# Six tiles of a chunked linear-attention stage in 64x64 matmul tiles, with their loads split by even and odd heads and the decay tables on GpSimd

## The chip, the cores and the metric

The kernel runs on one core of one Trainium2 chip. The time is the device time of one execution in microseconds (us). The engines are named as in the profile: PE is TensorE (matmuls), PEld its loading of weights, DVE is VectorE, ACT is ScalarE, POOL is GpSimd, and SP is SyncE, which only issues DMAs. L316 is line 316 of the kernel before; a line of the changed kernel is named as such.

## The reference

Two stages follow each other. The first is a linear attention with decay over 768 tokens, for 4 batches and 8 heads of 64 dimensions; the second is a feed-forward layer with a sine inside, on all 3072 tokens:

```python
gamma = 1.0 - 2.0 ** (-5.0 - np.arange(H))          # one decay per head
for t in range(S):
    state = gamma * state + outer(k[t], v[t])        # (64 x 64) per batch and head
    y[t] = scale * q[t] @ state
...
x = y as (3072 tokens, 512)                          # heads side by side
h = x @ w_in                                         # 512 -> 2048
g = h + sin(alpha * h) ** 2 / alpha
out = g @ w_out                                      # 2048 -> 512
```

Inputs and output are float32; the matmuls work on bf16.

## The kernel before

**Tiles.** The attention is computed in chunks of 128 tokens: 6 per batch, 24 tiles in all. Inside a chunk the decay is brought into tables, so that three kinds of matmul remain: *scores* (keys times queries, masked to the causal half), *values* (masked scores times values, plus queries times the state that the earlier chunks left), and the *state* (keys times values, added to the running sum). The order of the 24 tiles is written out: first the four first chunks of the four batches (tiles 1 to 4), then batch by batch the other five chunks. So tiles 5 to 9 are chunks two to six of batch 0, tile 10 is the second chunk of batch 1, and the 14 tiles from 11 on are all later ones. They go to the second stage in eleven groups: the first four tiles together, then two at a time.

**Two ways to compute a tile.** Tiles 11 to 24 are *wide*: their queries, keys and values lie with 64 tokens on each half of the partitions, four heads on each half, and all their matmuls are 64x64 (64 rows of contraction, 64 output rows), four of which fit into the PE array. `burst` (L391) issues them: `inter` (queries times state, L344), `scores` of the next tile (L355, L359), `sums` (the state, L374) and `mix` (values, L387). `mix` adds into the same PSUM as `inter` from other array rows, so an empty PE instruction in front of it waits for the last product of `inter`. DVE then masks the next tile's scores (L364), takes the outputs out with the decay table (`leave`, L414) and adds the state to its float sum (`keep`, L421); ACT, or POOL in batch 3, copies that sum to bf16 for the next tile (`hand`, L427).

Tiles 5 to 10 are not wide: all 128 tokens lie on the partitions. `stage_A` (L267) gives scores in 8 matmuls of 64 rows by 128 output rows (L273), and one DVE operation masks them (L277). `stage_M` (L305) multiplies queries with a block-diagonal copy of the state (`s_bd`, 128 rows by 64, L316), adds the values (L320) and, in `stage_S` (L280), adds the state into one PSUM bank that keeps it from tile to tile (L287). DVE takes the output out (L327, one operation of 128x512), and ACT copies the state's two diagonal blocks to `s_bd` (L303). When the first wide tile follows, `turned` (L291) changes the places of the heads in the state.

**Loads.** Every chunk load is issued by POOL (L84: 128 tokens x 8 heads x 64, cast to bf16 on the way), each of q, k and v by itself, and so are the weights (`w_in` in four pieces, L119; `w_out` in four, L122) and the wide tiles' loads, one per head (L109). The order in which POOL issues them is written out in the program. Queries and keys are turned by PE for the first tiles and for tiles 5, 6 and 8 (`stage_T`, L254; copied out by ACT or DVE), for the other tiles by a DMA transposition that SP issues (`turn`, L264). The values are scaled with their decay by `scale_v` (L143), on DVE for tiles 5 and 6 and on POOL for the others.

**Decay tables.** `qg` has a table of 128x512 floats for each chunk number; ACT makes the first, and `decay_table` (L220) multiplies it into the other five on DVE: three at 14.9 us, one each in slots 0 and 4 of phase 1.

**Second stage and order.** A `Slot` (L442) is a group of first-layer products: for a group of two tiles 8 products of 256 columns (L456), ACT's two sines (L459), a square on ACT (L464) or DVE (L466), and DVE's two additions into `gT` (L471). The products with `w_out` (L481, *output products*) follow one group later. `phase(g)` runs the eight slots of group g; in each slot it issues the slot's products, then what the dictionary `atts` has put there for attention tiles, then some output products of the group before, then the additions. Each engine takes its own instructions in that order. In PSUM, the slots and the output products share four banks (tag "mm"), and the attention's outputs have the banks "ps" and "ty".

Group 0 is written out by hand with tiles 4, 5 and 6 in it. There `fill(n)` issues n output products, 32 of which remain for the tiles 3 and 4: 16 are placed before phase 1 and 16 in it. Before phase 1 stand the scores of tiles 5 and 6, the first state (`SK(e0)`), and `stage_M` of both. In phase 1, slot 0 has tile 8's transposition, slot 1 tile 7's scores, slot 3 tile 7's `stage_M` and tile 8's scores, slot 6 tile 8's and tile 9's. Phase 2 has tile 9 in slot 1, with the scores of tile 10 and the first state of batch 1, and tile 10 in slot 5 with the first wide scores.

Of the kernel before, what the change touches and what calls it, by code (L numbers as in the profile page):

```python
# [8 lines left out]
F32 = mybir.dt.float32  # L9
# [7 lines left out]
def kernel(  # L17
# [15 lines left out]
    nc = tc.nc  # L33
# [35 lines left out]

    def chunk_of(t, j):  # L70
        b, c = divmod(j, NCH)
        return t[b, :, c * C:(c + 1) * C, :].rearrange("h s d -> s h d")

    def load_chunk(j, names="qkv"):
        for name, src in (("q", q), ("k", k), ("v", v)):
# [8 lines left out]
            nc.gpsimd.dma_start(out=t, in_=chunk_of(src, j))  # L84
# [4 lines left out]

    def spot(h):  # L90

        return h // NP, (h % NP) ^ (h // NP)

    def load_seq(bt, names="qkv"):
# [7 lines left out]
        for name, src in (("q", q), ("k", k), ("v", v)):  # L102
            if name not in names:
                continue
            for h in range(H):
                b, at = spot(h)
                r = slice(64 * b, 64 * b + 64)
                o = tv[r, :, at, :] if name == "v" else tqk[r, :, "qk".index(name), at, :]
                nc.gpsimd.dma_start(out=o, in_=src[bt, h, cs[0] * C:, :].rearrange("(f i) d -> i f d", i=64))  # L109
# [44 lines left out]
    load_w_in(3)  # L154
    load_w_out(2)
    load_w_out(3)
    for j in order[4:7]:
        load_chunk(j)
# [36 lines left out]
    def later_tables():  # L195
        for b in range(2):
# [3 lines left out]
            for e in range(2):  # L200
                nc.vector.tensor_copy(lgq[r, e::2], lg[r, NP * b + (e ^ b):NP * b + NP:2])
# [17 lines left out]
    def decay_table(c):  # L219
        nc.vector.tensor_mul(qg[:, c], qg[:, 0], step[:, c, :, None].to_broadcast([128, NP, C]))  # L220
# [5 lines left out]
    s_bd = [big.tile([128, NP, 128], BF16, name=f"s_bd{i}") for i in range(2)]  # L226
# [53 lines left out]
    def stage_S(j):  # L280
        c = j % NCH
        if c == 0:
            st["ps"] = psum.tile([128, NP, D], F32, name="ps", tag="ps")
        ps = st["ps"]
        for p in range(NP):
            for e in range(2):
                nc.tensor.matmul(ps[64 * e:64 * e + 64, p, :], raw["k", j][:, 2 * p + e, :], raw["v", j][:, 2 * p + e, :],  # L287
                                 start=(c == 0 and p == 0), stop=True, skip_group_check=True)
        return ps

    def turned(to, ps, copy):  # L291

        copy(to[:, 0:2], ps[:, 0:2])
        for e in range(2):
            copy(to[64 * e:64 * e + 64, 2:4], ps[64 - 64 * e:128 - 64 * e, 2:4])

    def keep_S(j, ps):
        if wide(j + 1):
            turned(s_q[(j % NCH + 1) % 2], ps, nc.scalar.copy)
            return  # L300
        for e in range(2):
            r = slice(64 * e, 64 * e + 64)
            nc.scalar.copy(s_bd[(j % NCH + 1) % 2][r, :, r], ps[r, :, :])  # L303

    def stage_M(j):  # L305
        c = j % NCH
# [3 lines left out]
        qkT, aT, vs = st["qkT", j], st["aT", j], raw["v", j]  # L310
        py = psum.tile([128, NP, 128], F32, name="py", tag="ty")
        if c > 0:
            for p in range(NP):
                for e in range(2):
                    r = slice(64 * e, 64 * e + 64)
                    nc.tensor.matmul(py[r, p, :], s_bd[c % 2][:, p, r], qkT[:, p, :],  # L316
                                     start=(p == 0), stop=True, skip_group_check=True)
        for p in range(NP):
            for e in range(2):
                nc.tensor.matmul(py[64 * e:64 * e + 64, p, :], vs[:, 2 * p + e, :], aT[:, e, p, :],  # L320
                                 start=(c == 0 and p == 0), stop=True, skip_group_check=True)
        x = xT[g][:, :, i * C:(i + 1) * C]
        if c == 0:
            nc.scalar.copy(x, py)
            return
        ps = stage_S(j) if c < NCH - 1 else None
        nc.vector.tensor_mul(x, py, qg[:, c])  # L327
        if ps is not None:
            keep_S(j, ps)

    def half(x):
        return slice(64 * x, 64 * x + 64)
# [3 lines left out]
    def inter(j):  # L338
# [3 lines left out]
        for m in range(2):  # L342
            for b, e in tiles4:
                last = nc.tensor.matmul(st["py", j][b][half(e ^ b), m * 128:(m + 1) * 128].rearrange("p (f i) -> p f i", f=2),  # L344
                                        s[half(e), 2 * b + m, :], qkT[half(e), m:m + 5:4, half(b)],
                                        start=(m == 0), stop=True, skip_group_check=True)
        return last

    def scores(j):

        qkT = st["qkT", j]
        pa = st["pa", j] = psum.tile([128, 2, 512], F32, name="pa", tag="pa")
        for m in range(2):
# [8 lines left out]
        aT = work.tile([128, 2, 2, 192], BF16, name="aTw", tag="aT", bufs=2)  # L362
        st["aT", j] = aT
# [3 lines left out]
    def sums(now, to, lo):  # L367

        ks, vs = raw["k", now], raw["v", now]
        for f in range(2 if wide(now) else 1):  # L370
            for m in range(2):
                for b, e in tiles4:
                    h = 4 * b + 2 * m + (e ^ b)
                    nc.tensor.matmul(to[b][half(e), lo + 64 * m:lo + 64 + 64 * m],  # L374
                                     ks[half(b), f, 2 * m + e, :] if wide(now) else ks[:, h, :],
                                     vs[half(b), f, 2 * m + e, :] if wide(now) else vs[:, h, :],
# [435 lines left out]
```

## Time and profile before

| | us |
|---|---|
| median of 3 runs | 213.54 (213.53 to 214.42) |
| profiled execution, of which | 213.53 |
| its span | 211.7 |
| phase 1 with the first slot of phase 2 | 48.10 to 63.97 |
| the next eight slots | 63.97 to 79.34 |
| the eight after them | 79.34 to 95.04 |

A line of the timeline has a start in us from the span's start, the busy time, the engine, the line of the kernel, the operation, output <- inputs, partitions x elements with their types, and the number of instructions that were merged; in brackets stands how long the engine was idle ahead of it and what it waited for. For PE, a name such as 64\*128 is rows by columns of the array that a matmul takes. A busy time of several merged matmuls runs to the end of the last one, while the next may start behind the last one's start. In a row of busy time by stage stand the stretch, its length, and the busy times of PE, PEld, DVE, ACT and POOL with their instruction counts, then the granted clock of PE, the DMA share and GB/s. The granted clock is 1.00 all through.

### The profile page before, as it was taken

What the parts mean: (1) busy time and instruction counts of PE and PEld (TensorE: products, weight loads), DVE (VectorE), ACT (ScalarE), POOL (GpSimd) and SP (SyncE); (2) the same over time, 40 slices, a digit from 0 to 9 for tenths busy, and PEclk for the clock granted to TensorE, in tenths of its full rate; (3) what the DMA queues carried; (4) which work ended last, traced back from release to release, by engine and by line L of the source; (5) the groups of instructions that cost most, each with busy time, mean ns of one, the idle gap of its engine ahead of it and who ended that gap; (6) DMA issues with size and microseconds to landing.
All of it is one profiled execution on the core that took longest, in us unless ns stands there. A gap on an engine that the chain in (4) does not pass through costs nothing.

```text
span 211.7 us, 5581 instructions
## 1 busy us (share of the span) xinstructions
PE 199.4 (94%) x2227; PEld 131.0 (62%) x2253; DVE 155.7 (74%) x353; ACT 157.7 (74%) x339; POOL 105.2 (50%) x140
## 2 busy tenths in 40 slices
PE   7798899899989999999999999999999999999994
PEld 3345454457766766766666667666666666666653
DVE  5877849966997688687777787777777878666550
ACT  7588696858887887877867877876876786788821
POOL 8975434977989649699799951001021020000000
PEclk9999999999999999999999999999999999999999
DMA  8999999999997989999999994403513110110112
GB/s 124 154 198 186 206 207 173 154 148 240 142 152 71 166 129 159 113 133 140 140 182 167 193 127 104 99 24 79 88 38 81 54 48 5 50 50 3 50 50 99
DMA packets 101337, 25.00 MB, mean 118 GB/s; under 512 B 93872, under 2 KB 98368, under 8 KB 101312
## 3 DMA queue, kind: packets, MB, share of 16 engines
q0 software_dynamic: 77504, 13.38, 86.7%
q1 hardware_dynamic: 23664, 11.22, 26.3%
q8 instruction: 17, 0.28, 0.6%
q14 instruction: 8, 0.07, 0.1%
q10 hardware_dynamic: 144, 0.07, 0.1%
HBM read 27.27 MB, written 6.29 MB: 159 GB/s over the span
## 4 chain that ended last, share of the span: by engine, by line
PE 78%; DVE 14%; ACT 4%; issue 3%; ACTq 0%
PE po L481 33%; PE ph L456 31%; DVE gT L471 5%; DVE aT L277 4%; PE spare L525 3%; ACT s L459 2%; ACT s L464 2%; PE poh L506 2%; PE py L344 2%; PE py L387 1%; DVE s L466 1%; PE pa L273 1%; PE pa L355 1%; PE py L320 1%; PE pa L374 1%
## 5 line engine op out<-in xcount | busy, mean ns | idle before, releaser
L471 DVE SCALAR_TENSOR_TENSOR gT<-s,rec_alpha,ph 128x256 bf16<-128x256 f32 (+3 forms) x184 | 82.4, 489 | 36.0 <-ACT s L464 35.8
L459 ACT ACTIVATE s<-ph,alpha_sb 128x256 f32<-128x256 f32 (+3 forms) x184 | 79.3, 480 | 35.2 <-PE ph L456 34.5
L456 PE MATMUL ph<-xT,w_in 128*128 128x256 bf16 (+3 forms) x735 | 98.6, 277 | 0.3 <-DVE gT L471 0.2
L481 PE MATMUL po<-w_out,gT 128*128 128x512 bf16 x344 | 90.4, 379 | 4.8 <-issue 3.3
L456 PEld LDWEIGHTS <-w_in 128*128 128x128 bf16 x736 | 70.6, 98 | 30.6 <-issue 1.0
L464 ACT ACTIVATE s<-s 128x512 f32<-128x512 f32 (+1 forms) x92 | 57.1, 621 | 2.5
L481 PEld LDWEIGHTS <-gT 128*128 128x128 bf16 x368 | 33.8, 98 | 27.7 <-issue 1.2
L427 POOL CAST s_q<-s_f 128x256 bf16<-128x256 f32 x5 | 2.0, 397 | 43.3 <-DVE s_f L421 25.7
L143 POOL TENSOR_TENSOR v_seq<-v_seq,kgq 128x512 bf16<-128x512 bf16 x14 | 14.6, 1066 | 8.8 <-ACT s L459 4.9
L109 POOL DMA_DIRECT2D qk_seq<-in_q_dram x24 | 17.1, 743 | 3.2 <-DMA v_seq<-in_v_dram 1.7
L109 POOL DMA_DIRECT2D qk_seq<-in_k_dram x24 | 17.0, 731 | 2.4 <-DMA qk_seq<-in_q_dram 1.3
L109 POOL DMA_DIRECT2D v_seq<-in_v_dram x24 | 17.0, 756 | 0.0
L493 DVE COPY o_sb<-po 128x512 f32<-128x512 f32 x19 | 13.1, 692 | 5.2 <-PE po L481 5.2
L364 DVE TENSOR_TENSOR aTw<-pa,maskq 128x768 bf16<-128x768 f32 x14 | 13.3, 952 | 0.0
L84 POOL DMA_DIRECT2D vr<-in_v_dram x10 | 9.2, 924 | 3.3 <-DMA w_in<-in_moe_w_in_dram 1.7
L525 PE MATMUL spare<-warm 128*128 128x512 bf16 x27 | 9.2, 464 | 1.3 <-DVE warm L162 1.2
L414 DVE TENSOR_TENSOR xT<-py,qg 128x256 bf16<-128x256 f32 x28 | 10.5, 417 | 0.0
L84 POOL DMA_DIRECT2D qkr<-in_q_dram x9 | 8.1, 902 | 3.8 <-DMA w_in<-in_moe_w_in_dram 1.7
L84 POOL DMA_DIRECT2D qkr<-in_k_dram x9 | 8.1, 898 | 3.9 <-DMA w_out<-in_moe_w_out_dram 3.4
L143 POOL TENSOR_TENSOR vr<-vr,kg 128x512 bf16<-128x512 bf16 x7 | 7.4, 1072 | 1.4 <-DMA vr<-in_v_dram 1.4
L277 DVE TENSOR_TENSOR aT<-pa,mask 128x1024 bf16<-128x1024 f32 x6 | 7.3, 1218 | 0.4 <-PE pa L273 0.4
L277 DVE TENSOR_TENSOR aT<-pa,dec 128x1024 bf16<-128x1024 f32 x4 | 4.9, 1223 | 1.8 <-PE pa L273 1.8
(94 smaller groups left out, 141.5 us busy)
## 6 DMA issues: line engine op xcount, KB each, us to landing
out_dram<-o_sb SPq DMA_DIRECT2D x23, 256.0 KB, 2.8
w_in<-in_moe_w_in_dram POOLq DMA_DIRECT2D x4, 512.0 KB, 11.0
w_out<-in_moe_w_out_dram POOLq DMA_DIRECT2D x4, 512.0 KB, 14.8
vr<-in_v_dram POOLq DMA_DIRECT2D x10, 128.0 KB, 6.9
qk_seq<-in_q_dram POOLq DMA_DIRECT2D x16, 80.0 KB, 6.9
qk_seq<-in_k_dram POOLq DMA_DIRECT2D x16, 80.0 KB, 5.1
v_seq<-in_v_dram POOLq DMA_DIRECT2D x16, 80.0 KB, 5.5
qkr<-in_q_dram POOLq DMA_DIRECT2D x9, 128.0 KB, 7.0
```

Of the source, the lines that this page charges most:

```text
L84: nc.gpsimd.dma_start(out=t, in_=chunk_of(src, j))
L109: nc.gpsimd.dma_start(out=o, in_=src[bt, h, cs[0] * C:, :].rearrange("(f i) d -> i f d", i=64))
L143: eng.tensor_mul(t, t, by[:, j % NCH, :, None].to_broadcast([128, H, D]))
L277: nc.vector.tensor_mul(aT.rearrange("p e n t -> p (e n) t"), pa.rearrange("p e n t -> p (e n) t"), m)
L364: return {"mask": lambda: nc.vector.tensor_mul(aT, pa[:, :, 0:384].rearrange("p e (m t) -> p e m t", m=2), maskq[:, None, None, :].to_broa ...
L456: nc.tensor.matmul(self.ph[:, m, :], w_in[:, i, f * 128:(f + 1) * 128], xT[g][:, i, self.lo:self.hi], start=(m == 0 and i == 0), stop=(i = ...
L459: nc.scalar.activation(out=self.s[:, m, :], in_=self.ph[:, m, :], func=ACTF.Sin, scale=alpha_sb[:, f:f + 1])
L464: nc.scalar.activation(out=self.s, in_=self.s, func=ACTF.Square)
L471: nc.vector.scalar_tensor_tensor(gT[self.g][:, f, self.lo:self.hi], self.s[:, m, :], rec_alpha[:, f:f + 1], self.ph[:, m, :], op0=ALU.mult ...
L481: nc.tensor.matmul(po[g, ts], gT[g][:, f, ts * C:(ts + 1) * C], w_out[:, f, :], start=(f == 0), stop=(f == FF - 1))
L493: nc.vector.tensor_copy(o_sb, po[g, ts])
L525: nc.tensor.matmul(spare["ps"], warm[:, :128], warm, start=True, stop=True)
```

## The change

1. Tiles 5 to 10 go through `burst` too, in 64x64 matmuls. `head(b, m, e)` places a head by the three bits of its number, `inter` writes bank e instead of bank b, and the values and the state of these tiles are split by token half: `round_of(j, now, n)` issues, for one half on each array row, 8 value products (128 columns for the first token half, 64 for the second) and 8 state products (64 columns). Round 0 follows `inter`; then come the next tile's scores (16 products of 64x64 with 128 columns); then the empty PE instruction, which now waits for round 0's last product; then round 1.
2. The state is no longer kept in PSUM. DVE adds it to the float sum for each tile (`keep`), ACT copies it to bf16 (`hand`); `s_bd`, `turned`, `keep_S` and their copies go. The output leaves in two DVE operations of 128x256.
3. Queries and keys of tiles 5 to 10 are loaded in two halves, even heads and odd heads (128 tokens x 4 heads x 64 each).
4. The five tables are made by POOL, between the last weight loads and the loads of tiles 5 and 6. The loads of tiles 8, 9 and 10 are issued one tile after the other; tile 7's and tile 8's values are scaled by DVE in slots 1 and 4 of phase 1.
5. Tile 8's transposition stands before phase 1 (copied out by ACT); 20 output products are placed before phase 1 and 12 in it; all squares of phase 1 are ACT's; tile 7's scores move to slot 0. In the bursts of tiles 7 and 8 the state is added, and for tile 8 the output taken out, ahead of the next tile's mask.

```diff
+    def head(b, m, e):
+        return 4 * m + 2 * e + (e ^ b)
+    heads = [(b, m, e) for m in range(2) for b in range(2) for e in range(2)]
...
+            if name != "v" and spread(j):
+                for o in range(2):
+                    nc.gpsimd.dma_start(out=t[:, NP * o:NP * o + NP], in_=chunk_of(src, j)[:, o::2])
...
     def decay_table(c):
-        nc.vector.tensor_mul(qg[:, c], qg[:, 0], step[:, c, :, None].to_broadcast([128, NP, C]))
+        nc.gpsimd.tensor_mul(qg[:, c], qg[:, 0], step[:, c, :, None].to_broadcast([128, NP, C]))
...
+    def first_state(j):
+        ps = psum.tile([128, NP, D], F32, name="ps", tag="ps")
+        for b, m, e in heads:
+            h = head(b, m, e)
+            nc.tensor.matmul(ps[half(e), 2 * b + m, :], raw["k", j][:, h, :], raw["v", j][:, h, :],
+                             start=(b == 0 and m == 0), stop=True, skip_group_check=True)
+        nc.scalar.copy(s_q[1], ps)
+        nc.vector.tensor_copy(s_f, ps)
...
+        if not wide(j):
+            for p in range(NP):
+                for f, e in tiles4:
+                    nc.tensor.matmul(pa[half(f), e, 128 * p:128 * p + 128], qkT[half(e), NP + p, half(f)],
+                                     qkT[half(e), p, :], start=(p == 0), stop=True, skip_group_check=True)
...
+    def round_of(j, now, n):
+        py, aT, vs = st["py", j], st["aT", j], raw["v", j]
+        for b, m, e in heads:
+            f = e ^ n
+            last = nc.tensor.matmul(py[e][half(e ^ b), m * 128 + 64 * f:(m + 1) * 128], vs[half(f), head(b, m, e), :],
+                                    aT[half(f), e, 2 * (e ^ b) + m, 64 * f:],
+                                    start=False, stop=True, skip_group_check=True)
+        if now is not None:
+            ks, vs = raw["k", now], raw["v", now]
+            for b, m, e in heads:
+                f, h = b ^ n, head(b, m, e)
+                last = nc.tensor.matmul(py[b][half(e), 256 + 64 * m:320 + 64 * m],
+                                        ks[half(f), NP * (e ^ b) + 2 * m + e if spread(now) else h, :],
+                                        vs[half(f), h, :], start=False, stop=True, skip_group_check=True)
+        return last
...
     def burst(old, new, first=None):
...
+        last = inter(old)
+        if not wide(old):
+            last = round_of(old, now, 0)
         more = scores(new) if new is not None else {}
...
+        behind(last)
+        if wide(old):
+            mix(old)
...
+        else:
+            round_of(old, now, 1)
...
-    load_w_in(3)
-    load_w_out(2)
-    load_w_out(3)
-    for j in order[4:7]:
-        load_chunk(j)
...
+    for c, load in ((1, lambda: load_w_in(3)), (2, lambda: load_w_out(2)), (3, lambda: load_w_out(3)),
+                    (4, lambda: load_chunk(order[4])), (5, lambda: load_chunk(order[5]))):
+        decay_table(c)
+        load()
+    load_chunk(order[6])
...
-    stage_A(P[5])
     fill(2)
-    SK(e0)()
+    first_state(e0)
     scale_v(P[5], nc.vector)
     fill(4)
-    stage_M(P[4])
+    run(burst(P[4], P[5]), "keep", "hand", "mask", "exit")
+    fill(5)
+    stage_T(P[7], nc.scalar, "mm")
+    fill(3)
+    run(burst(P[5], None), "exit", "keep", "hand")
     fill(4)
-    stage_M(P[5])
-    fill(4)
-    where = {6: (1, 1), 7: (1, 3), 8: (1, 6)}
+    where = {6: (1, 0), 7: (1, 3), 8: (1, 6)}
...
+            more = burst(old, new, first)
+            if new in P[7:9]:
+                run(more, *(("exit",) if new == P[8] else ()), "keep")
...
+    for j, n in ((P[6], 1), (P[7], 4)):
+        at((1, n), lambda j=j: scale_v(j, nc.vector))
...
-    phase(1, outs, atts[1], 2, (2, 5))
+    phase(1, outs, atts[1], 2)
```

More of the change, by code (lines that the diff above doesn't have):

```diff
@@ L278, in stage_A, with x_of @@
         st["aT", j] = aT
[L280 to L306, printed above, removed]
+    def first_state(j):
[6 more added lines that the diff above has]
+        nc.vector.tensor_copy(s_f, ps)
+    def x_of(j):
         g, i = place[j]
@@ L689 @@
     F((0, 1), (12,))
-    stage_A(P[4])
+    scores(P[4])["mask"]()
     a.sq("A").add()
```

155 lines of the change are left out of this document (56 added, 99 removed).

## The prediction

> **What bounds the kernel now.** The profiled execution took 213.53 us: a span of 211.7 and 1.83 around it. The median of the three runs is 213.54 (213.53 to 214.42), so the sum below is made against 213.53 and holds for the median. A measurement of this kernel can tell about 0.5% (1.07 us) from no change. I read the busy line first, then busy time by stage, then the timeline around the changed tiles.
>
> ```profile
> PE 199.4 (94%) x2227; PEld 131.0 (62%) x2253; DVE 155.7 (74%) x353; ACT 157.7 (74%) x339; POOL 105.2 (50%) x140
> ```
>
> TensorE looks like the bound, but 94% is a mean over stages. By stage (columns: window, length, then busy time of PE, PEld, DVE, ACT, POOL), the first row is phase 1 with the first slot of phase 2, the others are the next two stretches of eight slots:
>
> ```profile
> 48.10:63.97 15.87, 15.00 (x170) 11.16 (x172) 14.16 (x26) 13.27 (x31) 13.60 (x19) 1.00 2.09 171
> 63.97:79.34 15.37, 15.05 (x163) 10.63 (x164) 11.04 (x23) 12.39 (x28) 10.52 (x14) 1.00 1.05 122
> 79.34:95.04 15.70, 15.38 (x209) 10.62 (x209) 12.46 (x30) 12.22 (x26) 14.00 (x20) 1.00 2.15 137
> ```
>
> From phase 2 on PE paces, and DVE and ACT have 3 us or more to spare: a microsecond that PE loses before 64 us is lost for good. Phase 1 is different. The timeline of DVE has no gap from 49.62 on, and at its end PE waits for it, then it waits for ACT:
>
> ```profile
> 61.06 1.22 DVE L277 TENSOR_TENSOR aT<-pa,mask 128x1024 bf16<-128x1024 f32 x1
> 62.20 1.66 DVE L471 SCALAR_TENSOR_TENSOR gT<-s,rec_alpha,ph 128x256 bf16<-128x256 f32 x4
> 64.86 0.87 DVE L471 SCALAR_TENSOR_TENSOR gT<-s,rec_alpha,ph 128x256 bf16<-128x256 f32 x2 [1.00 <-ACT s L464]
> ```
>
> PE's timeline at the same time:
>
> ```profile
> 63.11 1.02 PE L481 MATMUL po<-w_out,gT 128*128 128x512 bf16 x4 [0.40 <-DVE gT L471]
> ```
>
> So PE and DVE are within half a microsecond of each other there. That stage decides this change.
>
> **PE: the six tiles.** Tile 7 (value and state products), with tile 8's scores behind it, before:
>
> ```profile
> 53.87 0.41 PE L316 MATMUL py<-qkT,s_bd 128*64 128x128 bf16 x8
> 54.11 0.39 PE L320 MATMUL py<-aT,vr 128*64 128x128 bf16 x8
> 54.34 0.29 PE L287 MATMUL ps<-vr,qkr 128*64 128x64 bf16 x8
> 54.56 0.40 PE L273 MATMUL pa<-qkT 64*128 64x128 bf16 x8
> ```
>
> Two output products follow; the record of the first is missing (344 L481 products, 368 loads), so the next product starts one product (0.216 us) before the 55.12 shown, at 54.90: 1.03 us. What a 64x64 product costs is read from a wide tile:
>
> ```profile
> 81.17 0.31 PE L344 MATMUL py<-qkT,s_q 64*64 64x128 bf16 x8
> 81.31 0.23 PE L355 MATMUL pa<-qkT 64*64 64x128 bf16 x4
> 81.37 0.20 PE L359 MATMUL pa<-qkT 64*64 64x64 bf16 x4
> ...
> 81.48 0.30 PE L374 MATMUL pa<-v_seq,qk_seq 64*64 64x64 bf16 x16
> 81.61 0.34 PE L387 MATMUL py<-aTw,v_seq 64*64 64x128 bf16 x16
> ```
>
> Starts are 0.015 us apart for 128 columns (4 in 0.06) and 0.008 for 64 (16 in 0.13). The new burst: state 0.14; a round has 4 products of 128 columns and 12 of 64, 0.16; scores 16 of 128, 0.24; the other round 0.16; 0.12 to the next full-width product. The second round waits for the end of the first. In a burst with nothing between, the value products began 0.16 us after the last state product's end (104.78 to 104.94), so the distance from last start to next start is 0.19 + 0.16 = 0.35, of which the scores cover 0.24: 0.11 stays. PE takes its list in order, so all its later products stand behind that wait. Sum 0.93. Tiles 7, 8: -0.10 each. Tile 9, with the state product of the next batch inside, took 1.15 (64.94 to 66.09): -0.22. Tile 10: 1.00, now with wide scores 0.93: -0.07. Tiles 5 and 6, from 42.69 to 48.10, less 14 output products (3.02): 2.39; then first state 0.35, burst 0.1 + 0.93, burst without scores 0.1 + 0.14 + 0.16 + 0.35 + 0.16 + 0.12: 2.41. Together **-0.47 us**. SP's list keeps its order and length, and the wide tiles from 11 on issue as many products of the same shapes as before: 0. The bounds: every burst as short as a wide one (0.72; -1.6), or no gain (0).
>
> The Trainium skill (TensorEngine Tiling (Array Packing), Overview, Theoretical Speedup) gives up to 2x for one small side and up to 4x for both, so the changed products would halve. The rows agree only in part: 16 scores products take 0.24 us where 8 of double width took about as long, since those filled the array already. By the page, as an estimate, the four later bursts would give -2 us; rival 3 has what rows give.
>
> **Moved ahead of phase 1.** Tile 8's PE transposition (8 products, 0.44: 48.98 to 49.42) and four output products (0.86) now stand before phase 1, which keeps 12 output products of 16. On ACT one copy of the state (0.39) takes the place of two (0.36 each), which no product of PE waited for. New before tile 6's burst: it writes the two banks that tile 5's exit reads. DVE's order there is keep (pair 0.48, rows at 84.27), tile 6's mask (1.13), exit (pair 0.70, rows at 83.61). Keep starts 45.5, exit ends 47.9; PE arrives at 47.65 (five products, transposition, three products after 45.4): wait 0.3. Phase 1 then starts at 42.69 + 18 x 0.216 + 0.44 + 2.41 + 0.3 = 49.75, not 48.10.
>
> **Phase 1 on DVE.** Before, start to start: transposition copy 0.61, 16 gT 6.3 (pair 0.79), 3 masks 3.4, 2 squares 1.3, 2 exits 1.2, 2 tables 1.2: 14.0. After: 16 gT 6.3, 3 masks 3.4, 2 scalings 1.3 (rows 0.68 at 42.12 and 0.96 at 44.37), 2 keeps 1.0, 2 exits 1.4: 13.4. PE's own work falls more, to 8 x 0.87 + 12 x 0.216 + 0.45 + 2 x 1.03 = 12.1. DVE cannot start early: the first mask needs the scores behind slot 0 (51.2), and all squares are now ACT's (pitch 0.87 + 0.54 = 1.41), so slot 2's gT starts at 55.35. From there DVE has no gap: six gT pairs 4.8, two keeps 1.0, two masks 2.3, two exits 1.4, one scaling 0.6, to 65.4; before it was 63.86. Phase 1 keeps its length (15.6 against 15.8) while its start moved by 1.65: the moved PE work is paid twice, once ahead and once as waiting. PE waits for tile 8's scaling at 59.8 (0.3) and for a bank at 62.4 (the copy of the last phase-0 output, behind slot 7's square and the hand copy on ACT, ends 64.45). Slot 1 of phase 2 starts 65.4, slot 2 at 65.4 + 0.87 + 0.1 + 0.93 + 0.86 = 68.16; before 66.96. **+1.20**, and tile 10's burst -0.07: **+1.13**. (The -0.40 of tiles 7 to 9 is inside.) Bounds: without DVE's gaps ahead of 55.35, +0.3; with scalings at 0.96 and gT pairs at 0.87, +1.9.
>
> **POOL, tables and loads.** No row shows a float table on POOL; the nearest are DVE's (0.67) and POOL's bf16 scaling (1.07); up to double that for the bytes: 0.67 to 2.1, taken 1.1, at the POOL row. The tables delay no weights:
>
> ```profile
> 22.97 0.88 POOL L84 DMA_DIRECT2D vr<-in_v_dram  x1 [1.23 <-DMA w_out<-in_moe_w_out_dram]
> 25.50 0.87 POOL L84 DMA_DIRECT2D qkr<-in_q_dram  x1 [1.65 <-DMA w_in<-in_moe_w_in_dram]
> ...
> 36.62 0.87 POOL L84 DMA_DIRECT2D vr<-in_v_dram  x1
> ```
>
> Each issue starts when the load eight places before it has landed (22.97: the first w_out, 11.72 + 11.0 = 22.7; the same holds up to 35.67). POOL idles 13.2 us in these waits from 15 to 36 us. Five tables (5.5) and the six more issues of tiles 5 to 7 (each pair of halves 1.4 for 0.88: 3.1) fit into that, and the last weights land at 35.4 (18.77 + 16.6), so a later issue leaves no gap in the queue; at 2.1 a table the cover is just used up, and the load of tile 6, which landed 0.3 us ahead of its use (40.0, 40.31), would cost what it is late. The tables that DVE drops at 14.92 gain nothing: its next gT waited for ACT anyway (0.60). But a half load is one of eight in flight with half the bytes. The nearest issue is a 64 KB one (0.68 to 0.75 against 0.88), so a tile takes 4 x 0.7 + 0.88 = 3.7 us of POOL, not 2.6. By this tile 8's last k half is issued at 43.7; in 5.8 us (the slowest full load then) it lands at 49.5, at the 2.6 us of an unloaded 64 KB load at 46.3. PE needs it at 46.4 (before, it lands at 45.4 for 48.98). I take 47.4: of 1.0 us wait 0.3 lies under the bank wait, **+0.5**. For tile 11 the k loads end 4 us later; its DMA transposition (66.19 + 4.3 = 70.5 now) has 3.3 us to spare, then 0 to 1.5 late: **+0.2**.
>
> **Sum:** 213.53 + 1.13 + 0.5 + 0.2 = **215.4**.
>
> **Rivals.** (1) Loads decide: tile 8 lands 2.5 us late (+2.2) and tile 11 by 1.5: 213.53 + 1.13 + 2.2 + 1.5 = 218.4; half of that lateness gives 216.5. For it: the eight-in-flight rows, DMA engines at 9 tenths to 127 us. Against it: the queue is full until 35.4 and bytes are the same. The Trainium skill (DMA: Bandwidth & Descriptors, Rules for kernel authors) says to join small transfers, mostly overhead under 64 KB; the trace has 64 KB loads at 2.6 to 7 us, so it agrees in kind. 0.2. (2) DVE's lag is absorbed: gaps before 55.35 vanish because ACT's sines start right behind PE, and loads are in time: +0.3 to -0.5, 213.4. 0.25. (3) Not slower but faster: PE still paces phase 1, so DVE ends by 63.2; then all bursts at a wide tile's 0.72 give -1.3 for four and -0.3 for tiles 5 and 6, less the 0.4 idle at 62.7: -2.0, 211.5. It decides if slot 6's gT ends before PE reaches phase 2; rows make that 64.7 against 62.4. 0.12. (4) The products don't pack and nothing else moves: 213.9, inside (2).
>
> **Chances.** Forecast 0.43, (1) 0.2, (2) 0.25, (3) 0.12. Slower by over 0.5% 0.61 (forecast and (1), less 0.02 for its edge at 214.6), within 0.27, faster 0.12. The range takes the forecast, most of (1) and (2): 213.0 to 217.6; the forecast's own is 214.2 to 216.5.
>
> **What would show it.** Bursts of 0.9 us from state product to next output product; phase 1's first slot at 49.6 to 50.5; DVE without a gap from 55 to 65 and a PE wait over 1 us near 63, released by DVE or ACT; tile 8's transposition waiting for a DMA; phases 3 to 10 at 15.5 us each as now. Wrong if PE shows no wait in phase 1, or if a wait for a load is the longest.

## The result, and the profile after

The changed kernel took **220.0 us** (median of 4 runs, 219.95 to 220.98) against 213.53: a ratio of **1.0303 (95% interval 1.0264 to 1.0342)**. The forecast was 215.4 and the range ended at 217.6: the sign was right, the size was not.

The profiled execution has a span of 218.2 us. Its busy line, and the granted clock in 40 slices of 5.5 us:

```profile
PE 205.0 (94%) x2397; PEld 131.5 (60%) x2397; DVE 156.2 (72%) x361; ACT 157.4 (72%) x334; POOL 115.9 (53%) x155
...
PEclk9999999995899999999999999999999999999999
```

PE is 94% busy as before, and again that says nothing. The clock line, full throughout before, has a hole in the slices that hold 49 to 60 us. By stage (columns as in the prediction; the last three are granted clock, DMA share, GB/s):

```profile
41.56:55.33 13.77, 9.56 (x133) 4.63 (x133) 5.00 (x12) 3.67 (x7) 12.25 (x17) 0.77 1.73 162
55.33:70.86 15.53, 14.44 (x217) 10.37 (x216) 13.26 (x29) 13.40 (x31) 15.53 (x23) 0.98 1.60 123
70.86:86.14 15.28, 15.28 (x207) 10.57 (x206) 11.94 (x28) 11.40 (x25) 10.95 (x15) 1.00 1.39 147
```

Phase 1 (second row) and the stretch behind it are no longer than before (15.53 and 15.28 against 15.87 and 15.37). The loss stands in the first row, ahead of phase 1. PE's timeline there:

```profile
45.80 0.28 PE L259 MATMUL pt<-ident,qkr 128*128 128x128 bf16 x2
46.52 0.28 PE L259 MATMUL pt<-ident,qkr 128*128 128x128 bf16 x2 [0.45 <-DMA qkr<-in_q_dram]
48.29 0.29 PE L259 MATMUL pt<-ident,qkr 128*128 128x128 bf16 x2 [1.49 <-DMA qkr<-in_k_dram]
50.75 0.39 PE L259 MATMUL pt<-ident,qkr 128*128 128x128 bf16 x2 [2.17 <-DMA qkr<-in_k_dram]
50.94 1.49 PE L488 MATMUL po<-w_out,gT 128*128 128x512 bf16 x3
...
53.65 1.89 PE L488 MATMUL po<-w_out,gT 128*128 128x512 bf16 x4
55.33 1.28 PE L463 MATMUL ph<-xT,w_in 128*128 128x256 bf16 x8
```

Tile 8's transposition, moved ahead of phase 1, waits three times for its half loads, 4.11 us in all. Behind it everything is slow: four output products take 1.68 us (53.65 to 55.33) instead of 0.87. The windows of the wait and of what follows say why:

```profile
45.80:50.94 5.14, 1.03 (x9) 0.52 (x8) 1.29 (x3) 0.00 (x0) 4.34 (x6) 0.81 1.75 205
50.94:55.33 4.39, 4.31 (x50) 1.89 (x48) 1.15 (x4) 1.90 (x3) 3.67 (x5) 0.50 1.86 161
```

In the second, PE has work nearly without a gap, at a granted clock of 0.50.

Profiled executions differ by up to 0.8 us in when the first first-layer slot starts (15.23 to 16.01; before 15.97, after 15.26). So below two lengths are counted from it: to phase 1's first slot, and to the third slot of phase 2 ("the stage"; the prediction calls that slot 2). Before: 32.13 and 50.99. After: 40.07 and 58.30. The stage is **7.31 us longer**; what follows it is alike (144.74 and 144.64). The first slot of this execution started 0.71 us sooner, so the time rose by 6.47 only.

### The profile page after: what moved, and what is told of

Its sections match the earlier page's. It is cut to its first block, busy times and chain, and to the rows that moved or that the text cites. A ratio compares the mean times of both kernels' runs of the same rounds, so it can differ in the third digit from the quotient of the medians.

```text
span 218.2 us, 5900 instructions
## 1 busy us (share of the span) xinstructions
PE 205.0 (94%) x2397; PEld 131.5 (60%) x2397; DVE 156.2 (72%) x361; ACT 157.4 (72%) x334; POOL 115.9 (53%) x155
## 4 chain that ended last, share of the span: by engine, by line
PE 74%; DMA 14%; POOL 8%; issue 1%; ACT 1%; DVE 0%; POOLq 0%
PE po L488 33%; PE ph L463 32%; DMA w_out<-in_moe_w_out_dram 7%; DMA w_in<-in_moe_w_in_dram 4%; DMA qkr<-in_k_dram 3%; POOL qkr L98 3%; PE py L326 2%; POOL vr L100 2%; PE poh L513 2%; POOL qkr L100 2%; PE py L376 1%; PE py L385 1%; PE pa L343 1%; PE pa L360 1%; PE pa L336 1%
## 5 line engine op out<-in xcount | busy, mean ns | idle before, releaser
L488 PE MATMUL po<-w_out,gT 128*128 128x512 bf16 x368 | 97.0, 384 | 1.9 <-ACT o_sb L502 1.1
L471 ACT ACTIVATE s<-s 128x512 f32<-128x512 f32 (+1 forms) x94 | 58.6, 623 | 2.6
L488 PEld LDWEIGHTS <-gT 128*128 128x128 bf16 x368 | 34.4, 98 | 29.1 <-issue 2.7
L422 DVE TENSOR_TENSOR xT<-py,qg 128x256 bf16<-128x256 f32 x40 | 15.0, 418 | 6.7 <-PE py L392 6.7
L98 POOL DMA_DIRECT2D qkr<-in_k_dram x12 | 9.2, 790 | 4.6 <-DMA w_in<-in_moe_w_in_dram 2.1
L98 POOL DMA_DIRECT2D qkr<-in_q_dram x12 | 9.4, 807 | 3.2 <-DMA w_out<-in_moe_w_out_dram 1.7
L434 ACT CAST s_q<-s_f 128x256 bf16<-128x256 f32 x14 | 5.5, 392 | 4.0 <-DVE s_f L428 4.0
L259 PE MATMUL pt<-ident,qkr 128*128 128x128 bf16 x32 | 3.2, 225 | 4.3 <-DMA qkr<-in_k_dram 3.9
## 6 DMA issues: line engine op xcount, KB each, us to landing
w_out<-in_moe_w_out_dram POOLq DMA_DIRECT2D x4, 512.0 KB, 14.6
```

What stands on the lines that cost most here:

```text
L98: nc.gpsimd.dma_start(out=t[:, NP * o:NP * o + NP], in_=chunk_of(src, j)[:, o::2])
L422: nc.vector.tensor_mul(x[:, b::2, :], py[b][:, 0:256].rearrange("p (m t) -> p m t", m=2), qg[:, c, b::2])
L471: nc.scalar.activation(out=self.s, in_=self.s, func=ACTF.Square)
L488: nc.tensor.matmul(po[g, ts], gT[g][:, f, ts * C:(ts + 1) * C], w_out[:, f, :], start=(f == 0), stop=(f == FF - 1))
```

## The runs

Theory: split loads and the earlier need together starve tile 8's transposition, because POOL paces the loads by their number; the clock falls behind that wait; phase 1 costs about what was forecast. Rivals: the tables push the loads; the early transposition alone is at fault; the clock is a side show; the packed products cost more than they save.

| run | what it is | median us | ratio to before (95%) | to phase 1 | stage |
|---|---|---|---|---|---|
| after | the change | 220.00 | 1.0303 (1.0264-1.0342) | 40.07 | 58.30 |
| e1 | whole loads | 217.34 | 1.0199 (1.0059-1.0340) | 33.59 | 56.17 |
| e2 | transposition back in phase 1 | 217.21 | 1.0193 (1.0139-1.0247) | 34.14 | 53.73 |
| e3 | tables on DVE | 220.25 | 1.0336 (1.0296-1.0376) | 39.98 | 57.95 |
| e4 | spare products in the wait | 219.05 | 1.0280 (1.0239-1.0320) | 38.69 | 56.67 |
| e5 | before, half loads | 217.62 | 1.0177 (1.0142-1.0212) | 32.11 | 53.69 |
| e6 | before, transposition early | 215.37 | 1.0090 (1.0074-1.0107) | 33.43 | 52.90 |
| e7 | whole loads, transposition back | 216.03 | 1.0108 (1.0082-1.0134) | 34.61 | 54.17 |
| e8 | e7, scalings on POOL | 215.47 | 1.0116 (1.0075-1.0157) | 34.11 | 54.76 |
| e9 | e8, more outputs ahead, burst at 5 | 215.21 | 1.0084 (1.0064-1.0104) | 33.68 | 52.81 |
| e10 | whole, early, scalings on POOL | 214.28 | 1.0041 (1.0026-1.0056) | 33.67 | 51.80 |
| e11 | e10, scalings on DVE | 216.57 | 1.0133 (1.0092-1.0175) | 33.67 | 54.17 |
| e12 | e10, tile 7's scores at slot 0 | 214.00 | 1.0046 (1.0019-1.0073) | 35.04 | 53.26 |
| e13 | e10, burst at slot 6 | 214.35 | 1.0035 (1.0004-1.0066) | 33.82 | 51.52 |
| e14 | e10, state copied at once | 214.28 | 1.0033 (1.0009-1.0056) | 33.68 | 51.66 |
| e15 | e13 and e14 | 214.46 | 1.0032 (1.0004-1.0060) | 33.69 | 51.35 |
| e16 | e11, spare products in a wait | 215.89 | 1.0105 (1.0070-1.0140) | 34.06 | 54.11 |
| e17 | e15, last output earlier | 214.07 | 1.0033 (1.0011-1.0055) | 33.81 | 50.82 |
| e18 | before, last output earlier | 213.60 | 1.0006 (0.9977-1.0036) | 32.13 | 52.31 |

A ratio compares mean times with those of the kernel before, timed beside that run (medians 213.05 to 213.53). The two lengths are those of one profiled execution each.

**e1: whole loads**

```diff
-            if name != "v" and spread(j):
+            if False:
```

> Edit: tiles five to ten load q and k with one DMA each again (128 KB, heads in their old order in memory, so the products of these tiles pair the wrong heads: the time alone counts); every other instruction is that of the changed kernel. My theory (late halves): POOL paces the loads from 36 us on, at 0.77 us for 64 KB against 0.88 us for 128 KB; with one DMA each the last k load of tile 8 is issued near 41.6 instead of 43.85 and lands by about 46, so the 4.1 us of waiting in tile 8's transposition shrinks under 0.7, the granted clock in 50 to 60 us stays at 1.00 and the time is 213.0 to 214.5. Rival A (the tables on POOL push the loads): the waiting stays above 2.5 us and the time above 217. Rival B (the transposition is simply too early, whatever the loads): waiting of 1.5 us or more, 215.5 to 217.

The wait in the transposition is gone and phase 1 starts 6.5 us sooner, as the theory had it. The time was missed: 218.55 in the profiled execution, 216.13 in the other, whose mean clock was 1.00 against 0.992. Tile 7's DMA transposition came 1.12 us late for its scores, and a hole opened in tile 8's burst:

```profile
61.32 0.24 PE L392 MATMUL py<-vr,qkr 64*64 64x64 bf16 x2
64.35 0.23 PE L392 MATMUL py<-vr,qkr 64*64 64x64 bf16 x5 [2.78 <-issue]
...
64.73 1.45 PE L463 MATMUL ph<-xT,w_in 128*128 128x256 bf16 x8
65.98 1.06 PE L488 MATMUL po<-w_out,gT 128*128 128x512 bf16 x2
66.83 1.91 PE L463 MATMUL ph<-xT,w_in 128*128 128x256 bf16 x8
```

"issue" names no releaser; no other profile here has this hole, and its cause stays open. The two slots behind it take 1.25 and 1.72 us, start to next start, instead of 0.87: the clock again, 0.50 from 65.2 to 68.6.

**e2: transposition back in phase 1**

```diff
-    fill(5)
-    stage_T(P[7], nc.scalar, "mm")
-    fill(3)
+    fill(4)
...
+    at((1, 1), lambda: stage_T(P[7], nc.scalar, "mm"))
```

> Edit: tile 8's transposition goes back into phase 1, behind its second slot, and one output product fewer stands ahead of phase 1; half loads and tables stay. My theory: the last k half lands near 50.7 as now, PE reaches the transposition near 51, so the wait is under 0.7 us, the clock stays 1.00 in 50 to 60 us, and the time is 213.0 to 214.5 (220.0 less 4.1 of waiting and 2.4 of clock). Rival (the halves land so late that some other reader of tile 8 waits for them): a wait of over 1.5 us for tile 8 appears in phase 1, and the time is above 215.5.

No wait for tile 8, a clock of 1.00 everywhere, 4.57 of the 7.31 us gone. The time was missed by 2.7 us: other waits stood behind the one removed, a bank ahead of tile 6's burst, the end of phase 1, and tile 11's DMA transposition.

```profile
47.42 0.54 PE L326 MATMUL py<-qkT,s_q 64*64 64x128 bf16 x8 [1.17 <-DVE xT L422]
...
65.41 1.02 PE L488 MATMUL po<-w_out,gT 128*128 128x512 bf16 x4 [0.98 <-DVE gT L478]
...
76.97 0.25 PE L343 MATMUL pa<-qkT 64*64 64x128 bf16 x4 [1.35 <-DMA qkT<-qk_seq]
```

**e3: tables on DVE**

```diff
-        nc.gpsimd.tensor_mul(qg[:, c], qg[:, 0], step[:, c, :, None].to_broadcast([128, NP, C]))
+        nc.vector.tensor_mul(qg[:, c], qg[:, 0], step[:, c, :, None].to_broadcast([128, NP, C]))
...
```

> Edit: the five tables are made on DVE again (two behind the last masks of the first four tiles, one behind the first slot, two in DVE's idle time near 27 us), loads in the changed kernel's order with halves. My theory: POOL's issues wait for earlier landings until 35 us in either kernel (tile 6's last k load is issued at 35.4 and 35.7), so the tables only filled waiting: tile 8's last k half still lands at 50 to 51, the wait stays 3.5 to 4.3 us, the time 219.3 to 220.5. Rival A (tables push the loads): tile 8's last half lands 2 us earlier or more, 217.5 or less.

As the theory had it: waits of 3.5 us for k and 0.4 for q, 220.25. The rival falls: the tables do not push the loads.

**e4: spare products in the wait**

```diff
+        for m in range(80):
+            nc.tensor.transpose(pt[:, m % 8, :], warm[:, :128], ident)
...
```

> Edit: 80 spare transpositions of a constant tile (about 0.058 us each, 4.6 in all) stand right ahead of tile 8's transposition, so PE works while the halves are on their way; they compute nothing. My theory: the halves land when they did (50.7), the granted clock stays 1.00 in 50 to 60 us, and what the clock cost comes back: 217.3 to 218.0. Rival C (the clock falls for another reason than PE's waiting, or its price is small): clock again near 0.7 in 50 to 60 us, 219.5 to 220.5.

The windows of the spare and real transpositions, then of the seven output products and tile 6's burst:

```profile
47.29:52.21 4.92, 4.92 (x90) 4.92 (x89) 1.30 (x3) 0.00 (x0) 4.92 (x7) 1.00 1.73 228
52.21:54.68 2.47, 2.39 (x51) 1.22 (x49) 0.70 (x3) 1.50 (x2) 1.61 (x4) 1.00 2.30 146
```

The clock stays at 1.00, and the same products take 2.47 us instead of 4.39: **the clock cost 1.92 us** there, and 0.24 more in phase 1's first slots (57.11 - 55.33 = 1.78 against 1.54). The stage shrank by 1.63 only, the time by 0.95, less than expected: the spare products, which began 1.5 us later than the transposition had (47.29 against 45.80), ran on until 51.8, while the last half had landed at 51.2 (45.22 + 6.0).

**e5 and e6: the two causes, each alone, in the kernel before**

```diff
+            if name != "v" and j % NCH > 0 and not wide(j):
+                for o in range(2):
+                    nc.gpsimd.dma_start(out=t[:, NP * o:NP * o + NP], in_=chunk_of(src, j)[:, NP * o:NP * o + NP])
```

> The kernel before, with one edit: q and k of tiles five to ten are loaded in two DMAs of 64 KB each (heads 0 to 3, then 4 to 7); all else is as before. My theory (POOL paces the loads by their number): tile 8's last k half is issued 2 us later than before and lands at 48.5 to 51, PE needs it at 48.98, so the split alone costs 0 to 2 us in tile 8's transposition: the wait named for tile 8's k load is 0.3 to 2.0 us, and the time 0.2% to 1.0% above before. Rival (the split alone is fatal, its lateness is what the changed kernel shows at 4 us): a wait over 3 us and 2% or more. Rival (the split is free while PE's need is late): no wait for tile 8 at all and less than 0.2%.

```diff
     stage_M(P[4])
-    fill(4)
+    fill(5)
+    stage_T(P[7], nc.scalar, "mm")
+    fill(3)
...
-    at((1, 0), T(P[7]))
```

> The kernel before, with one edit: tile 8's transposition and four output products move ahead of phase 1, as in the changed kernel; loads are whole. My theory: the loads (last one at 45.4) are in time for it, no wait for a load; phase 1 starts 1.3 us later and, since DVE paces it, does not get all of that back: 0.1% to 0.6% above before. Rival (PE paces phase 1, the moved work comes back one for one): within 0.1%.

e5: no wait for tile 8's loads (the last landed at 49.0, just as PE came to it), so the wait that I expected did not come; yet 1.8%. Six pairs of issues push POOL's own later work, the scalings of tiles 8 and 9, which stand in the same queue (the stage is 2.70 us longer in this execution, the shortest of its four):

```profile
60.21 0.41 PE L324 MATMUL py<-aT,vr 128*64 128x128 bf16 x8 [0.90 <-POOL vr L147]
...
67.56 0.41 PE L324 MATMUL py<-aT,vr 128*64 128x128 bf16 x8 [1.13 <-POOL vr L147]
```

e6: 0.9%, more than expected, without a wait for a load: 1.30 us of PE work moved ahead of phase 1, and none of it came back. PE waited inside phase 1 instead:

```profile
59.72 1.03 PE L456 MATMUL ph<-xT,w_in 128*128 128x256 bf16 x8 [1.05 <-DVE gT L471]
...
65.04 1.02 PE L481 MATMUL po<-w_out,gT 128*128 128x512 bf16 x4 [0.76 <-ACT o_sb L495]
```

So neither part alone makes the 4 us; with whole loads the early need is met (e6), with the late need halves are in time (e5). Together they are not.

**e7 and e8: whole loads and the late transposition; then the scalings on POOL**

```diff
-        return j % NCH > 0 and not wide(j)
+        return j in order[6:10] and j != order[7]
...
+                for e in range(2 if j % NCH else 0):
+                    nc.tensor.transpose(pt[half(e), i * NP + p, :], raw["qk"[i], j][:, 4 * (p % 2) + p // 2 + 2 * e], ident)
...
```

> The changed kernel with two edits: tile 8's transposition back in phase 1, and tiles 5, 6 and 8 load q and k with one DMA each, heads in their old order (PE picks the heads by transposing 64 columns at a time; only the tiles that a DMA turns keep their halves). My theory: POOL has six issues fewer, so the waits for the turned tiles 7 and 11 (0.2 and 1.35 us with the transposition alone moved back) shrink under 0.5 together; what stays is the bank wait of tile 6's values (1.2) and the wait for DVE at the end of phase 1 (1.0): 0.7% to 1.4% above before. Rival (the changed products themselves cost more than they save): 1.7% or more above before without a wait for a load over 0.5 us.

```diff
+    scale_v(P[6], nc.gpsimd)
...
+    scale_v(P[7], nc.gpsimd)
...
-    for j, n in ((P[6], 1), (P[7], 4)):
-        at((1, n), lambda j=j: scale_v(j, nc.vector))
```

> As the kernel with both edits (transposition back in phase 1, whole loads for tiles 5, 6 and 8), and the scalings of tiles 7 and 8 move from DVE, inside phase 1, to POOL, between its loads: 1.3 us of DVE work less in phase 1. My theory (DVE paces phase 1): PE's wait at its end (1.0 us) falls under 0.4, and the time is 0.3 to 0.6% below that of the kernel without this edit. Rival (the end of phase 1 waits for ACT's copy of the last output of phase 0): the wait stays at 0.7 us or more, less than 0.2% of difference. Rival (POOL's work delays loads): a wait for a turned tile over 1 us takes its place.

e7 as expected, its waits 1.16 (bank) and 1.01 (end of phase 1). e8 cannot be told from e7 (1.0116 against 1.0108): the wait at the end of phase 1 stayed at 0.98, as the first rival had it, but what ends it is DVE's gT, not a copy of ACT. The likely reason is DVE's order: slot 6's gT, whose bank PE waits for, stands behind the exit, sum and mask of tile 8's burst; in e9, with that burst a slot earlier, the wait is gone. e8's profiled execution (217.25; the other three 215.26 to 215.50) shows the clock once more, behind a bank wait of 1.46 us:

```profile
47.91 0.54 PE L329 MATMUL py<-qkT,s_q 64*64 64x128 bf16 x8 [1.46 <-DVE xT L425]
...
49.00 1.30 PE L491 MATMUL po<-w_out,gT 128*128 128x512 bf16 x4
50.09 1.92 PE L466 MATMUL ph<-xT,w_in 128*128 128x256 bf16 x8
```

**e9 to e12: place of the transposition, of the burst, of the scalings**

```diff
-    fill(4)
+    fill(9)
...
-    where = {6: (1, 0), 7: (1, 3), 8: (1, 6)}
+    where = {6: (1, 0), 7: (1, 3), 8: (1, 5)}
```

> The kernel with whole loads for tiles 5, 6 and 8, tile 8's transposition in phase 1 and the scalings of tiles 7 and 8 on POOL, and two more edits: nine output products instead of four stand between the value products of tile 5 and those of tile 6, and tile 8's burst stands behind slot 5 instead of slot 6 of phase 1. My theory (a wait for a PSUM bank ahead of tile 6 of 1.2 to 1.5 us, and the work that tile 8's burst gives DVE just ahead of phase 1's end, are what is left of the loss): the first wait falls under 0.4 us, the one at the end of phase 1 under 0.5, the time is 213.3 to 214.6. Rival (DVE's whole work in phase 1 is the bound, wherever it stands): the waits move, the time stays at 215 or more.

For e10 the transposition stands early again and the line reads {6: (1, 1), 7: (1, 3), 8: (1, 5)}.

> The changed kernel's early transposition of tile 8, with whole loads for tiles 5, 6 and 8, the scalings of tiles 7 and 8 on POOL, tile 7's scores behind slot 1 instead of slot 0, and tile 8's burst behind slot 5 instead of slot 6. My theory: whole loads are in time for the early transposition (wait under 0.5), which fills the bank wait ahead of tile 6; the time is 213.0 to 214.4. Rival (work moved ahead of phase 1 is not given back, as in the kernel before with the early transposition alone): 214.8 or more, with over 1 us of waits for DVE or ACT in phase 1 and no wait for a load.

> As the kernel with the early transposition, whole loads, tile 7's scores behind slot 1 and tile 8's burst behind slot 5, but the scalings of tiles 7 and 8 stay on DVE in phase 1 (1.3 us of DVE work more there). My theory (DVE paces phase 1): 0.2 to 0.6% above the version with the scalings on POOL, the difference standing as waits for DVE in phase 1. Rival (DVE has room there): within 0.15%.

> As the kernel with the early transposition, whole loads, the scalings on POOL and tile 8's burst behind slot 5, but tile 7's scores stand behind slot 0 as in the changed kernel. My theory: tile 7, whose halves a DMA turns, is ready near 51 to 51.7, PE needs it at 50.6, so a wait of 0.2 to 1.1 us stands there; DVE's first mask comes no sooner for it; 0.1 to 0.4% above the version with the scores behind slot 1. Rival (the earlier mask helps DVE more than the wait costs): 0.1% or more below it.

e9: both waits went, but tile 8's burst now waits 0.87 us for the state's copy on ACT; the time stayed above 215, as the rival had it. e10 met the theory: **with whole loads the early transposition costs no wait**, and 6.50 of the 7.31 us are gone. e11 is 2.3 us above e10, far more than expected: its waits (0.99 and 0.55) were followed by a clock of 0.50 from 61.6 to 65.0. One of its four executions kept a mean clock of 1.00; it took 215.25 us, the others 216.51 to 217.14.

```profile
59.33 0.54 PE L329 MATMUL py<-qkT,s_q 64*64 64x128 bf16 x8 [0.99 <-DVE xT L425]
60.41 0.30 PE L388 MATMUL py<-aT,vr 64*64 64x128 bf16 x8 [0.55 <-DVE vr L154]
...
61.63 1.92 PE L466 MATMUL ph<-xT,w_in 128*128 128x256 bf16 x8
```

e12 cannot be told from e10, so neither its theory nor its rival is shown; its long stage is 1.2 us of waiting for tile 5's loads in that one execution.

**e13 to e18: is there a gain behind the waits?**

e13 puts the burst back at slot 6; e14 runs "hand" with "keep" right behind the burst; e15 does both; e16 is e11 with seven spare products ahead of tile 8's burst. e17 (on e15) and e18 (on the kernel before) have this:

```diff
-            while done < no * (n + 1) * nf // FF:
+            while done < no * (n + (2 if g == 1 else 1)) * nf // FF and done < no:
```

> The version with the early transposition, whole loads for tiles 5, 6 and 8 and the scalings on POOL, with tile 8's burst behind slot 6 again instead of slot 5: the state's copy has a slot more, so PE's wait for it (0.8 us) goes. My theory: 0.2 to 0.5% below the version with slot 5 if DVE's work behind the burst does not hold up phase 2; 213.0 to 213.9. Rival (DVE's work at the end of phase 1 costs as much): a wait of 0.7 us or more for DVE or ACT at the first output product of phase 2, 214.0 or more.

> The version with tile 8's burst behind slot 5, and the copy of the state for tile 8 stands right behind its sum instead of behind the next slot's sines on ACT. My theory: the copy ends 1.5 us earlier, the wait of 0.8 us goes, 213.0 to 213.9. Rival (ACT stands still for the sum and the sines come later): another wait of 0.5 us or more for ACT or DVE, 214.0 or more.

> Both: burst behind slot 6 and the copy right behind the sum. My theory: no gain over the better of the two single edits (the same wait is taken away), within 0.2% of it. If the changed products themselves gain what their bursts show (0.85 us for 1.03 to 1.15), the best of the three is 0.1 to 0.4% below the kernel before; if not, all three are at or above it.

> The version with the early transposition, whole loads, tile 8's burst behind slot 5 and the scalings on DVE, with seven spare products (1.5 us, they compute nothing) ahead of tile 8's burst, where PE waited 0.99 for DVE and 0.55 for the scaled values. My theory (the clock falls behind these waits and costs as much as they do): the granted clock stays 1.00 in 55 to 66 us and the time falls by 0.8 to 1.5 us, to 215.1 to 215.8. Rival (the time is DVE's, the clock only follows): 216.3 or more.

> The version with both edits on tile 8's burst (behind slot 6, state copied right behind its sum), whole loads for tiles 5, 6 and 8, scalings on POOL and early transposition; new: the output products of phase 0 left for phase 1 are spread so that the last stands behind slot 6 instead of slot 7, and its bank comes free before phase 2 asks for one. My theory: the wait of 1.0 us falls under 0.3, and the time falls by 0.5 to 0.9 us, to 213.0 to 213.9; relative to the kernel before 0.4% below to 0.2% above. Rival (DVE's gT behind the burst's mask is the real holder of the bank): the wait stays over 0.6 us and the time within 0.2 us of the version without this edit.

> The kernel before with the same edit alone (the last output product of phase 0 stands behind slot 6 of phase 1). My theory: its wait of 0.40 us at the first output product of phase 2 goes, 0 to 0.2% below before. Rival (DVE's work in phase 1 is the bound and the wait moves): within 0.05%, or above before.

In e13, e14 and e15 the wait of 0.80 us for the copy went and another of 1.06 (ACT), 0.80 (DVE's exit, at the same burst) and 1.02 (DVE) took its place, as the rivals of e13 and e14 had it; all three stay 0.3% above before, so by the condition set for e15 the changed products do not gain as a whole what their bursts show. e16 kept the clock at 1.00 but overshot the wait: its time fell by 0.68 us, short of the 0.8 that I expected, and its stage is e11's (54.11 and 54.17), so e16 does not part the clock from DVE. e17 took away the last wait (0.24 left of 1.02), and its stage, 50.82, is the only one below that of before, by 0.17. It then lost 0.82 us to tile 11's DMA transposition, and its time, 214.07, ended just above my range:

```profile
63.10 1.02 PE L491 MATMUL po<-w_out,gT 128*128 128x512 bf16 x4 [0.24 <-ACT o_sb L505]
...
74.26 0.25 PE L346 MATMUL pa<-qkT 64*64 64x128 bf16 x4 [0.82 <-DMA qkT<-qk_seq]
```

e18 cannot be told from before: the wait of 0.40 us went, and one of 1.05 for DVE's gT stands inside phase 1 instead (59.90), as its rival had it. No version here is shown to be faster than the kernel before.

## Why the prediction was wrong

The step that failed is the one on loads: "I take 47.4: of 1.0 us wait 0.3 lies under the bank wait, +0.5" (by these figures 0.7, not 0.5). It was mis-sized twice.

1. **The landing.** The last k half landed at 50.7, above my upper end of 49.5. Its issue came as worked out (43.80 against 43.7). What failed is the time from issue to landing: I took 3.7 us, with 5.8 at most as "the slowest full load then", and it was 6.9. The rows of before had more: the k load issued at 45.66 took 6.8 us and tile 8's own, issued at 38.42, 7.0; 43.7 + 7.0 is 50.7. Tile 8's last k load, its issue and the us to its landing, whole (e1) and as halves (after):

```profile
38.83 0.88 POOL L100 DMA_DIRECT2D qkr<-in_k_dram  x1
qkr<-in_k_dram POOLq DMA_DIRECT2D x1, 128.0 KB, 7.1
...
43.07 1.57 POOL L98 DMA_DIRECT2D qkr<-in_k_dram  x2
qkr<-in_k_dram POOLq DMA_DIRECT2D x1, 64.0 KB, 6.9
```

The half took as long as the whole, so what the split moved is the issue, by 5 us. From 25 to 36 us POOL's loads mostly wait for an earlier landing each, about one in 2.5 us in both kernels: the issue at 35.67 is tile 7's k before, the one at 35.42 tile 6's first k half after. From there on POOL has no gap in the changed kernel (36 to 44 us, after, then before):

```profile
36.00:40.00 4.00, 4.00 (x45) 2.19 (x44) 3.47 (x6) 3.44 (x5) 4.00 (x7) 1.00 1.78 113
40.00:44.00 4.00, 3.52 (x35) 1.46 (x36) 2.73 (x5) 2.38 (x4) 4.00 (x7) 1.00 1.63 104
...
36.00:40.00 4.00, 3.94 (x31) 2.03 (x31) 3.47 (x6) 3.26 (x6) 3.86 (x5) 1.00 2.45 152
40.00:44.00 4.00, 3.43 (x34) 1.59 (x34) 3.57 (x5) 2.70 (x4) 2.19 (x4) 1.00 2.51 154
```

The bytes come at 104 to 113 GB/s; before it was 152 and 154. An issue of 0.76 us for 64 KB is 86 GB/s, one of 0.88 us for 128 KB 149 GB/s: with halves the rate is POOL's. The Trainium skill's rule that I cited (DMA: Bandwidth & Descriptors, Rules for kernel authors: join small transfers) is borne out by e1 and e10, where tile 8's last whole k load landed at 46.0 and 45.0. Not settled: why tile 8's two k halves took 5.2 and 6.9 us to land where the halves issued from 37.7 to 41.6 took 3.0 to 3.5, and why in e5 the same halves, issued 0.3 us later, took 4.1 and 4.9 and had landed by 49.

2. **The clock.** It is in no term, since no row of before was under 1.00. It cost 1.92 + 0.24 us (e4) in the profiled execution. The mean clock of the other three was 0.992 instead of 0.984 at the same time (219.95 to 220.98); how their waits fell no trace shows.

"Loads decide", my rival 1, was the right mechanism at 0.2; its price of 2.2 us for tile 8 should have been 4.1 + 2.2, and tile 11, which it had 1.5 late, showed no wait, since PE itself was late. The forecast's own sign of being wrong, "if a wait for a load is the longest", came true: 2.17 us, against 1.06 in phase 1.

The other steps:

- Phase 1's start: 1.65 later was forecast; with the loads in time it is 1.46 (e1) to 1.69 (e13). Right. The stage then adds up: 1.5 + 4.1 + 1.9 ahead of phase 1 and, from there to the stage's end, 18.23 (0.24 of clock in it) against 18.86, -0.6: 6.9 of 7.31; 0.4 is not accounted for.
- Phase 1 itself: forecast 18.41 for that length, measured 18.23. "Moved PE work is paid twice" is shown by e6 in the kernel before (1.30 moved, 1.9 lost). In e17, without the wait at its end, phase 1 starts 1.68 later but takes 1.85 less (17.01), so there the moved work came back. In the changed kernel rival 2, the lag absorbed, falls. The wait near its end, over 1 us by DVE or ACT: 1.06 in after, for ACT.
- Bursts: forecast 0.93, measured 0.85 (tile 7: 60.48 to 61.33, to the next output product). The second round began 0.28 us behind the start of the first one's last products (60.75 to 61.03), not 0.35. Rival 3 falls: 0.72 was not reached, and the best stage of all runs (e17, whose other edits count too) is 0.17 us under that of before.
- Tables: 1.05 to 1.18 us each on POOL (taken 1.1), hidden (e3). Right.

## What to carry to other kernels

Before work is moved ahead of a stage, put the landing of each of its inputs beside its new start, and count what paces the issues: where POOL needs 0.76 us to start a load of 64 KB and 0.88 for one of 128 KB, splitting loads cuts the rate by two fifths. Take the time from issue to landing from the rows of the loads beside it, the slowest included. Price a wait of PE with the clock behind it, not alone. A wait taken away shows the next one: here waits of 0.8 to 1.5 us stood in turn at five places, and only a run showed which.

## What was not expected of the hardware

- **The clock falls to half behind short waits.** Waits of 4.11 (after), 2.78 (e1), 1.46 (e8) and 0.99 + 0.55 us (e11) were followed by a clock of 0.50: for 3.4 us in e1, e8 and e11, for 6.8 in after (48.99 to 55.81, the end of the wait included). Waits of 1.17 and 1.35 (e2) and 1.16 us (e7) were not, nor was one of 1.51 us at 21.13 in e4, so the length of one wait does not decide alone. In the 3.4 us ahead of each fall PE was busy for 0.9 to 1.9 us; the rows of e11:

```profile
58.15:61.56 3.41, 1.69 (x59) 1.14 (x59) 3.22 (x8) 2.29 (x5) 3.41 (x5) 1.00 1.88 118
61.56:64.98 3.42, 3.42 (x16) 2.28 (x15) 2.83 (x7) 1.37 (x3) 3.42 (x6) 0.50 1.53 100
```

In e8 and e11 the executions with such a stretch (mean clock 0.99) took 1.3 to 2.0 us more than those without (1.00); what else differed between them no trace shows. The Trainium skill (TensorE: Matmul & The Clock Gate, Why this matters for your kernels) warns of idle gaps over about 3 us, back to half rate. The half rate agrees; in e8 one wait of 1.46 us stood ahead of it.
- **DVE is held up while POOL makes float tables.** rec_alpha's first step took 0.17 us before and the scaling behind it 0.68; beside POOL's tables (13.98 to 15.16 and 15.90 to 16.96 in after):

```profile
13.83 1.38 DVE L572 TENSOR_SCALAR rec_alpha<-alpha_sb 128x16 f32<-128x16 f32 x1
...
15.41 2.11 DVE L154 TENSOR_TENSOR vr<-vr,kg 128x512 bf16<-128x512 bf16 x1
```

In after, e1, e2, e4 and e8 the first step began at 13.8 to 14.6 and ended within 0.1 us of the end of POOL's first table; in e3, without tables on POOL, it took 0.25 us. In e1, e2, e4 and e8 no table ran beside the scaling, and it took 0.63. DVE's next gT waited for ACT anyway, so it cost nothing here. The Trainium skill (SBUF — State Buffer, SBUF: two separate sides) has one port pair that DVE and GpSimd hold in turn for a whole instruction, which these rows fit.
